# Dealing the rows of the attention's stacks into six pieces of 16 and one of 12

## The chip, the core and the metric

The kernel runs on one core of one Trainium2 chip. The time is device microseconds (us) of one launch of the whole program. The kernel before was timed three times: median 711.07 us, from 707.58 to 716.1 us. One more execution was recorded by the hardware profiler; the engines are PE (matmul), DVE (vector), ACT (scalar), POOL (GpSimd) and SP, which computes nothing here and only issues transfers (DMAs).

## The reference

Two independent halves are computed and laid side by side.

Half A is attention with a memory, on x of 2048 tokens by 576 features, with 32 heads of 18 features. The tokens are cut into 4 segments of 512. Within a segment each head does a causal softmax attention; from the second segment on, the result is mixed with what a running memory M, z of the earlier segments gives.

```python
q = heads(x @ wq); k = heads(x @ wk); v = heads(x @ wv)      # 32 heads of 18
for s in range(4):
    logits = einsum("bhqd,bhkd->bhqk", qs, ks) * scale + mask
    a_dot = einsum("bhqk,bhkd->bhqd", softmax(logits), vs)
    a_mem = einsum(phi(qs), M) / (einsum(phi(qs), z) + 1e-6)
    o = g * a_mem + (1 - g) * a_dot
    M += einsum(phi(ks), vs); z += sum(phi(ks))
out_A = concat(o) @ wo
```

Half B is a spectral filter on another x of the same size: a two-dimensional real FFT, a product with complex weights, and the inverse FFT.

## The kernel before, in words

The program has four stages, and its order of work on every engine is written out by hand (a manual schedule): what an engine gets to do is what stands next in program order.

1. **Forward FFT** of half B (`FFT.forward`), while the weights of half A are loaded and split.
2. **Projections** (`ATT.projections`, L541): for each segment g = 0..3 thirteen units. Units 0 to 8 (`qk_unit`, L467) compute 128 rows of q or k each and split them into three bf16 parts (high, middle, low). The store at L494 puts these into memory as `qkD[g]`, of 1152 rows (576 of q, then 576 of k; head h has rows 18h to 18h+17) by 3 parts by 512 tokens. Units 9 to 12 (`v_unit`, L504) compute v for 128 tokens each and store it as `vD` (L518) from `vt`, a tile of two buffers. A unit is a generator: its later steps run in later iterations, so unit 8's store to `qkD` is issued in iteration 10, and the stores to `vD` in iterations 10, 11, 12 and after the loop. Between the units the middle of the FFT runs on DVE and ACT, with its weights loaded by SP (L238). In segment 3, `hook` (L1099) also begins the inverse stage's loads on POOL and, from `q0`, the loads of the first stacks.
3. **Inverse FFT** (`FFT.inverse`, L287): matmuls at L300 and L311, stores `yb` at L320. `ATT.prologue` (L906) is interleaved: it loads the stacks of the next groups and computes the first ten rounds of `s1`.
4. **Attention** (`ATT.attention`, L928): 133 steps t. In step t, `s1(t+10)` (L637) finds the row maxima for one head of each token half, `s2(t)` (L680) computes the exponentials, and `pv` (L709) multiplies by v. Eight steps treat one group n = 0..15 (8 heads of one segment).

A **stack** is the operand of the logits' matmuls: the q (or k) of 8 heads with its bf16 parts laid one under the other in 108 of a tile's 128 partition rows, 6 parts of 18 rows, each row 8 heads by 512 tokens. There are 3 buffers for q (`Qs`) and 4 for k (`Ks`); the first of each lies in a tile called `x0`, which the profile shows as `x`. Rows 108 and 109 are written elsewhere. `stack_dmas(n,qk)` (L619) makes the loads of one stack, one per part: SP DMAs at L628, each of 18 rows times 8 heads times 512 bf16, 144 KB, read from `qkD` in runs of 1 KB. There are 32 stacks, so 192 such loads.

They are issued one by one: `hook` pops 12 of them in segment 3 of the projections (L1108), `prologue` pops 31 entries at L917, and `attention` appends 6 + 6 + 1 entries per group at L954 to L956 and pops one at L976 and one at L1005 of every step. `s1` of group n+2 begins at step 8n+6, the loads of q for that group are appended at step 8n, and those of k for group n+3 behind them. A load of a stack must wait until the last matmul that reads the buffer's old content is done. SP issues in order: whatever a DMA waits for, all later ones on SP wait too. The list `qu` (stores of the attention's results at L729 and L734, popped beside `q`) and single loads (L763, L804 and others) go through the same engine.

Of the kernel before, what the change touches and what calls it, by code (L numbers as in the profile page):

```python
# [87 lines left out]
class Pace:  # L88

    def __init__(s,total): s.left=total; s.acc=0.0; s.q=[]  # L90
# [256 lines left out]
BF=mybir.dt.bfloat16  # L347
# [42 lines left out]
class ATT:  # L390
    def __init__(s,nc,tc,io,cp,dp):
        s.nc,s.tc,s.io=nc,tc,io
        s.ident=cp.tile([128,128],F32,name="ident"); s.bm=cp.tile([126,7,19],F32,name="bm")
        s.Mst=[None]+[cp.tile([126,5,126],F32,name=f"Mst{i}") for i in range(1,4)]
        s.zst=[None]+[cp.tile([126,5,32],F32,name=f"zst{i}") for i in range(1,4)]
        d=lambda n,sh,dt: dp.tile(sh,dt,name=n)
        s.qkD=[d(f"qkD{i}",[1152,3,512],BF) for i in range(4)]
        s.pqD=[None]+[d(f"pqD{i}",[576,512],F32) for i in range(1,4)]
        s.vD=[d(f"vD{i}",[4,128,622],F32) for i in range(4)]
        s.dp=dp  # L400
# [103 lines left out]
    def v_unit(s,g,tb,tp,pp):  # L504
        nc=s.nc
        P=[]
        for hf in range(2):
            ps=pp.tile([128,288],F32,name="pjv",tag="pj")
            yield from s.passes(ps,g,"wv",slice(288*hf,288*hf+288),slice(128*tb,128*tb+128),True)
            P.append(ps)  # L510
            yield
        vt=tp.tile([128,622],F32,name="vt")
        vv=vt[:,:608].rearrange("p (h c) -> p h c",c=19)
        nc.gpsimd.memset(vv[:,:,18:19],1.0)  # L514
        nc.gpsimd.memset(vt[:,608:],0.0)
        for hf in range(2):
            nc.scalar.copy(vv[:,16*hf:16*hf+16,:18],P[hf].rearrange("p (h c) -> p h c",c=18))
        nc.sync.dma_start(s.vD[g][tb],vt)  # L518
        if g==3: return
        for _ in range(3): yield  # L520
        if tb==0: s.pm=[pp.tile([126,3,7,19],F32,name=f"pm{i}",tag="pm") for i in range(2)]
        for t in range(5):
            w=7 if t<4 else 4; r=18*w
            nc.tensor.matmul(s.pm[t//3][:r,t%3,:w].rearrange("p h c -> p (h c)"),s.pk[:,tb,126*t:126*t+r],vt[:,133*t:133*t+19*w],  # L524
                start=tb==0 and t%3==0,stop=tb==3,skip_group_check=True)
        if tb<3: return
        yield
        n=g+1
        for t in range(5):
            w=7 if t<4 else 4; r=18*w  # L530
            m=tp.tile([126,7,19],F32,name="mm")
            nc.vector.tensor_tensor(m[:r,:w],s.pm[t//3][:r,t%3,:w],s.bm[:r,:w],op=OP.mult)
            M=s.Mst[n][:r,t,:r].rearrange("p (h c) -> p h c",c=18)
            z=s.zst[n][:r,t,:w]
            if n==1:
                nc.gpsimd.tensor_copy(M,m[:r,:w,:18])
                nc.gpsimd.tensor_copy(z,m[:r,:w,18])
            else:
                nc.gpsimd.tensor_tensor(M,m[:r,:w,:18],s.Mst[g][:r,t,:r].rearrange("p (h c) -> p h c",c=18),op=OP.add)
                nc.gpsimd.tensor_tensor(z,m[:r,:w,18],s.zst[g][:r,t,:w],op=OP.add)  # L540
    def projections(s,xp,tp,pp,wv,pace,hook):  # L541

        live=[]
        s.nid=wv.tile([128,128],BF,name="nid"); s.nc.scalar.activation(s.nid,s.ident,AF.Copy,scale=-1.0)
        lw=s.load_w("wv",576,wv,xp,288,"xl",4)
        def advance():
            for l in list(live):
                try: next(l)
                except StopIteration: live.remove(l)
        tot=pace.left-8  # L550
        for g in range(4):
            if g<3: xq=[s.xprep(g+1,t,(xp,s.x0)[g%2],xp,[128,512],"xst",2) for t in range(5)]
            for i in range(13):
                u=s.qk_unit(g,i,tp,pp) if i<9 else s.v_unit(g,i-9,tp,pp)
                if i==4 and g<3: s.pk=tp.tile([128,4,576],F32,name="pk",bufs=1)
                next(u)
                hook(g,i)
                next(lw,None); next(lw,None)
                if g<3 and i in (4,6,8,10,12): next(xq[(i-4)//2])
                if g<3 and i in (1,3,5,7,9): next(xq[(i-1)//2])  # L560
                w=tot/(36-18*.3+12*2.7+4*2.0)*((2.7 if g<3 else 2.0) if i>8 else .7 if s.third(g,i) else 1.0)
                advance()
                pace.take(w*.7)
                advance()
                next(u)
                pace.take(w*.3)
                live.append(u)
        while live: advance()
# [50 lines left out]
    def stack_dmas(s,n,qk):  # L619

        nc=s.nc; g,G=divmod(n,4)
        L=[]
        T,base,order=((s.Qs[n%3],0,(0,0,0,1,1,2)),(s.Ks[n%4],576,(0,1,2,0,1,0)))[qk]
        for pc,o in enumerate(order):
            a=s.qkD[g][base+8*G*18:base+8*G*18+18,o]
            ap=bass.AP(tensor=a.tensor,offset=a.offset,ap=[[1536,18],[1536*18,8],[1,512]])
            def go(T=T,pc=pc,ap=ap):
                nc.sync.dma_start(T[18*pc:18*pc+18],ap)  # L628
                if pc==5: s.loaded.add((n,qk))
            L.append(go)  # L630
        return L
    def load_v(s,n):
# [273 lines left out]
    def prologue(s):  # L906

        nc,io=s.nc,s.io
        yield
        s.masks()  # L910
        s.load_v(0)
        q=s.stack_dmas(1,0)+s.stack_dmas(1,1)+s.stack_dmas(2,0)+s.stack_dmas(2,1)+[lambda: s.load_v(1)]+s.stack_dmas(3,1)
        for i in range(2): yield
        i=0
        for t in range(10):
            for _ in s.s1(t):
                for _ in range(1+(i%24==0)):  # L917
                    if q: q.pop(0)()
                i+=1
                yield  # L920
            if 2<=t<6: nc.gpsimd.dma_start(s.Ks[t-2][108:110].rearrange("p h c -> p (h c)"),io["neg1"])
            if t in (3,7): m=s.mpath(t//4); next(m)
            if t in (4,8): next(m); next(m,None)
        assert not q
# [151 lines left out]
def emit(nc,tc,io):  # L1076
    def pool(es,name,bufs=1,**kw):
        return es.enter_context(tc.tile_pool(name=name,bufs=bufs,reuse_waits="tile",**kw))
    with ExitStack() as L0:
# [9 lines left out]
        with tc.manual_schedule():  # L1089
            x0=pool(L1x,"x0")  # L1090
            with ExitStack() as es:
                xp=pool(es,"xf",2); cf=pool(es,"cf"); st=pool(es,"st",2)
                pf=es.enter_context(PP(tc,"pf",dict(f1=3,c1=2)))
                F.forward(xp,cf,pf,A.load_w("wqk",1152,wq,st,576,"wst",3),A.first(Slots(x0),xp),A.consts)
            with ExitStack() as es:
                wv=pool(Rv,"wv"); xp=pool(es,"xp"); tp=pool(es,"tp",2); fwp=pool(es,"fw",2)
                pp=es.enter_context(PP(tc,"pp",dict(pj=5,pt=1,pm=2)))
                F.pace.add(F.middle(fwp)); F.pace.add(F.last())
                def hook(g,i):  # L1099
                    if g==3 and i==9:  # L1100
                        Rw.close()
                        tc.swap_default_side()
                        F.yp=pool(Ri,"yp",2); F.Yt={}; ci=pool(Ri,"ci")
                        tc.swap_default_side()
                        F.inv_setup(ci)
                    if g==3 and i>9: F.ysplit(i-10,nc.vector)
                    if g==3 and i==0: q0.extend(A.stacks0(x0))
                    for _ in range((0,2,2,2,2,1,1,1,1)[i] if g==3 and i<9 else 0): q0.pop(0)()  # L1108
                q0=[]
                A.projections(xp,tp,pp,wv,F.pace,hook)  # L1110
            Rv.close()
            with ExitStack() as L1:
                cp2=pool(L1,"cp2"); sm=pool(L1,"sm",2); sp=pool(L1,"sp",3)
                ps1=L1.enter_context(PP(tc,"ps1",dict(s1=3)))
                A.begin(sm,sp,ps1)
                with ExitStack() as es:
                    pi=es.enter_context(PP(tc,"pi",dict(i2=2,i3=2,mt=1)))
                    yl=pool(es,"yl",2)
                    A.att_setup(cp2)
                    A.psm,A.mtag=pi,"mt"  # L1120
                    pr=A.prologue(); next(pr)
                    for i,_ in enumerate(F.inverse(yl,pi)):
                        if i>5 and i%4!=3: next(pr,None)
                    for _ in pr: pass
                Ri.close(); Rz.close()
                with ExitStack() as es:
                    tp=pool(es,"tp2",2); ps=es.enter_context(PP(tc,"ps",dict(s2=3,pv=1,post=1)))
                    A.attention(tp,ps)
            L1x.close()
# [18 lines left out]
```

## Time and profile before

| what | value |
|---|---|
| median of 3 runs | 711.07 us (707.58 to 716.1) |
| the profiled execution's own time | 710.93 us |
| its span, first to last instruction | 709.2 us |
| PE busy | 676.4 us, 95% of the span |
| DVE, ACT, POOL busy | 556.2, 441.0, 208.8 us |
| granted PE clock | 0.997 |
| moved by DMA | 121.04 MB, mean 171 GB/s |

The span leaves out 1.7 us of launch and end. A core has 16 DMA engines; "DMA share" is their mean busy share, so one engine always busy is 1/16. In the list of waits a row reads: engine and line that waited, what it waited for, us in total, times, longest. In the table of stretches each engine has its busy time and, in brackets, its number of instructions; the last three columns are the granted clock, the DMA share and GB/s. "SPq" is SP's instruction queue; its duration is that of issuing, not of the transfer. A wait for several things is put down to the one that came last by the profile.

### The profile page before, as it was taken

Reading aid. Unit: us, or ns where it says so; the run is one execution under the profiler, and the core shown is the slowest. Engines: PE = TensorE matmul, PEld = TensorE weight load, DVE = VectorE, ACT = ScalarE, POOL = GpSimd, SP = SyncE. Lnnn points to the kernel's source line nnn. Section 1 sums busy time; section 2 is a strip of 40 time slices with the busy share of each in tenths; the row PEclk is TensorE's granted clock in tenths of the full one; section 3 lists DMA queues with packets and bytes.
Section 4 is the critical chain, followed back from the end, with each engine's and each line's share of the span. In section 5 each row is a group of like instructions: output and inputs, shape, how many; then the busy total and the mean of one; then the engine's idle time right before and its main releaser. Section 6 shows DMA issues by size and latency. Waiting matters only on the chain.

```text
span 709.2 us, 14168 instructions
## 1 busy us (share of the span) xinstructions
PE 676.4 (95%) x4861; PEld 498.7 (70%) x4861; DVE 556.2 (78%) x1233; ACT 441.0 (62%) x994; POOL 208.8 (29%) x409
## 2 busy tenths in 40 slices
PE   4999999999999999999999899999999999998997
PEld 4999779889879888999844444444566445764677
DVE  6999999899989889887588688877666876568153
ACT  3657695574574563444388677777666676567741
POOL 2110000100100111565165334555233753246210
PEclk9999999999999999999999999999999999999999
DMA  9876546555563568899647666676556765441331
GB/s 343 272 233 205 150 141 194 175 178 167 165 211 133 165 215 279 201 239 211 180 109 176 172 161 154 173 181 169 128 129 185 171 164 128 122 129 52 99 100 69
DMA packets 83388, 121.04 MB, mean 171 GB/s; under 512 B 11368, under 2 KB 50902, under 8 KB 83180
## 3 DMA queue, kind: packets, MB, share of 16 engines
q1 hardware_dynamic: 76724, 104.11, 51.8%
q0 software_dynamic: 6592, 16.03, 8.2%
q8 instruction: 38, 0.62, 0.4%
q14 instruction: 34, 0.28, 0.1%
HBM read 81.78 MB, written 38.24 MB: 169 GB/s over the span
## 4 chain that ended last, share of the span: by engine, by line
PE 61%; DVE 9%; DMA 6%; ACT 5%; issue 3%; POOL 3%; DVEq 0%; SPq 0%; ACTq 0%; POOLq 0%
PE pv L718 9%; PE po L861 7%; PE pj L464 6%; PE pjv L464 6%; PE s L644 5%; PE i L300 4%; PE i L311 4%; PE s L652 3%; PE s L688 3%; PE po L892 2%; DVE junk L648 2%; PE s L692 2%; PE pn L791 2%; PE pm L524 2%; PE s L653 2%
## 5 line engine op out<-in xcount | busy, mean ns | idle before, releaser
L648 DVE CUSTOM_DVE_ANT_0 junk<-s,mask 128x512 bf16<-128x512 f32 (+1 forms) x256 | 141.8, 554 | 55.1 <-PE s L644 44.3
L654 DVE TENSOR_REDUCE mx<-s 128x4 f32<-128x512 f32 x128 | 87.9, 687 | 20.0 <-PE s L653 18.2
L689 ACT ACTIVATE P<-s 128x512 f32<-128x512 f32 x128 | 77.2, 603 | 24.1 <-PE s L688 20.9
L718 PE MATMUL pv<-P,vs 128*32 128x512 f32 (+3 forms) x1024 | 82.3, 440 | 0.0
L694 ACT ACTIVATE P<-s 128x512 f32<-128x512 f32 x128 | 77.1, 602 | 6.9 <-PE s L693 3.8
L698 ACT ACTIVATE P<-s 128x256 f32<-128x256 f32 x128 | 49.6, 387 | 49.7 <-PE s L697 49.6
L701 POOL TENSOR_SCALAR_AFFINE_SELECT P<-P 128x512 f32<-128x512 f32 x116 | 69.4, 635 | 5.6 <-ACT P L689 4.7
L718 PEld LDWEIGHTS pv<-P,vs 128*32 128x32 f32 x1024 | 26.9, 109 | 45.0 <-issue 42.9
L464 PE MATMUL pj<-x,wqkh 128*128 128x512 f32 x162 | 56.1, 407 | 0.0
L210 DVE TENSOR_TENSOR t<-Z 128x580 f32<-128x580 f32 x64 | 46.7, 757 | 0.2
L514 POOL MEMSET vt<- 128x32 f32 x16 | 2.4, 159 | 148.8 <-PE pm L524 121.5
L210 DVE TENSOR_TENSOR Z<-t 128x580 f32<-128x580 f32 x64 | 45.9, 756 | 0.0
L644 PE MATMUL s<-Ks,Qs 108*128 108x512 bf16 (+1 forms) x128 | 42.2, 330 | 0.0
L488 ACT CAST sp<-pj 128x512 bf16<-128x512 f32 x36 | 21.1, 585 | 30.7 <-DVE pj L484 30.7
L142 PE MATMUL f<-ftab,eh 128*128 128x290 f32 (+1 forms) x160 | 31.6, 317 | 9.0 <-DMA ftab<-ftab 9.0
L300 PE MATMUL i<-civ,Y 128*128 128x256 f32 (+1 forms) x288 | 37.9, 284 | 1.6 <-DVE T L332 1.6
L300 PEld LDWEIGHTS i<-civ,Y 128*128 128x128 f32 (+1 forms) x288 | 35.8, 181 | 1.8 <-DVE T L332 1.8
L311 PE MATMUL i<-itab,T 128*128 128x290 f32 (+1 forms) x224 | 36.4, 312 | 0.0
L464 PEld LDWEIGHTS pj<-x,wqkh 128*128 128x128 f32 x162 | 30.4, 188 | 8.4 <-issue 1.7
L669 POOL CAST mh<-mg 128x16 bf16<-128x16 f32 x32 | 6.8, 214 | 99.1 <-ACT mg L667 67.9
L464 PE MATMUL pj<-xh,wqkh 128*128 128x512 f32 x90 | 35.6, 395 | 0.0
L464 PE MATMUL pj<-xh,wqkl 128*128 128x512 f32 x90 | 35.6, 395 | 0.0
(214 smaller groups left out, 1859.6 us busy)
## 6 DMA issues: line engine op xcount, KB each, us to landing
qkD<-sp SPq DMA_DIRECT2D x36, 384.0 KB
Ks<-qkD SPq DMA_DIRECT2D x72, 144.0 KB
x<-qkD SPq DMA_DIRECT2D x60, 144.0 KB
Qs<-qkD SPq DMA_DIRECT2D x60, 144.0 KB
xin<-xb SPq DMA_DIRECT2D x16, 384.0 KB
cfw<-cfw POOLq DMA_DIRECT2D x16, 384.0 KB, 4.5
civ<-civ POOLq DMA_DIRECT2D x16, 384.0 KB, 7.5
vs<-vD SPq DMA_DIRECT2D x16, 330.0 KB
```

The costliest lines, as they stand in the source:

```text
L210: v.tensor_tensor(o,a,b,op=op)
L300: nc.tensor.matmul(p[:m,k],Y[i][:,q,c*128:c*128+m],cc[:,hl,o:o+256],start=n==0,stop=n==5)
L311: nc.tensor.matmul(p,x,t,start=n==0,stop=n==6)
L464: s.nc.tensor.matmul(out,a,b,start=i==0,stop=i==len(L)-1)
L644: nc.tensor.matmul(out,Q[:108,h,128*i:128*i+128],K[:108,h,:128*(i+1)],start=True,stop=True)
L648: nc.vector.tensor_tensor_reduce(out=junk[:,:w],in0=src,in1=s.mask[:,512-w:],scale=1.0,scalar=-3.0e38, op0=OP.add,op1=OP.max,accum_out=s.m ...
L654: nc.vector.tensor_reduce(out=s.mx[k][:,hh],in_=pa.rearrange("p (b c) -> p b c",c=128),axis=mybir.AxisListType.X,op=OP.max)
L689: nc.scalar.activation(P[0][:,hh],p0,AF.Exp,scale=SC)
L694: nc.scalar.activation(P[1][:,hh],p1,AF.Exp,scale=SC)
L701: if k<29: nc.gpsimd.affine_select(out=x,in_=x,pattern=pat+[[1,128]],compare_op=OP.is_ge,fill=0.0,base=0,channel_multiplier=-1)
L718: nc.tensor.matmul(s.pvt[32*hh:32*hh+32,128*j:],vt[:,j,19*h:19*h+32],mv[0][:,hh,mv[1]],start=j==0,stop=j==2,skip_group_check=True)
L861: nc.tensor.matmul(ps,a[t][:r,c],b[:r,t,w],start=i==0,stop=i==14)
```

## The change

A stack's six parts of 18 rows are dealt in another way: rows 0 to 15 of each part go to a piece of 16 partition rows, and the two rows left of each part, 12 in all, to a seventh piece of 12 rows. The 108 rows keep their places in q and k alike, so the sums over them are the same.

The two left-over rows of a head lie in `qkD` far from those of the other parts. They are therefore gathered in memory into a new array `reD[g]` (64 rows of 12 by 512) by `rest(g)`: 12 copies from memory to memory per segment, six for q and six for k, of 32 heads by 2 rows by 512 bf16 each. SP issues the first six at the head of iteration 11 of the projections and the other six at the head of iteration 12. The seventh piece of a stack is loaded from `reD`. The pops are adapted: two more in `hook`, a pace of `1+(i%5==0)` in place of `1+(i%24==0)` in the prologue; in the attention, the 15 entries of a group go at the same pace of two a step.

```diff
+        s.reD=[d(f"reD{i}",[64,12,512],BF) for i in range(4)]
...
+    def rest(s,g):
+
+        L=[]
+        for qk in (0,1):
+            for pc,o in enumerate(((0,0,0,1,1,2),(0,1,2,0,1,0))[qk]):
+                a=s.qkD[g][576*qk+16:576*qk+17,o]; b=s.reD[g][32*qk:32*qk+32]
+                x=bass.AP(tensor=a.tensor,offset=a.offset,ap=[[1536*18,32],[1536,2],[1,512]])
+                y=bass.AP(tensor=b.tensor,offset=b.offset+512*2*pc,ap=[[512*12,32],[512,2],[1,512]])
+                L.append(lambda x=x,y=y: s.nc.sync.dma_start(y,x))
+        return L
...
+            rest=s.rest(g)
             for i in range(13):
+                for _ in range(6 if i>10 else 0): rest.pop(0)()
...
-        for pc,o in enumerate(order):
-            a=s.qkD[g][base+8*G*18:base+8*G*18+18,o]
-            ap=bass.AP(tensor=a.tensor,offset=a.offset,ap=[[1536,18],[1536*18,8],[1,512]])
+        for pc,o in enumerate(order+(0,)):
+            if pc<6:
+                a=s.qkD[g][base+8*G*18:base+8*G*18+18,o]
+                ap=bass.AP(tensor=a.tensor,offset=a.offset,ap=[[1536,16],[1536*18,8],[1,512]])
+            else:
+                a=s.reD[g][32*qk+8*G:32*qk+8*G+8]
+                ap=bass.AP(tensor=a.tensor,offset=a.offset,ap=[[512,12],[512*12,8],[1,512]])
             def go(T=T,pc=pc,ap=ap):
-                nc.sync.dma_start(T[18*pc:18*pc+18],ap)
-                if pc==5: s.loaded.add((n,qk))
+                nc.sync.dma_start(T[16*pc:16*pc+(16 if pc<6 else 12)],ap)
+                if pc==6: s.loaded.add((n,qk))
...
-                for _ in range(1+(i%24==0)):
+                for _ in range(1+(i%5==0)):
...
-                    for _ in range((0,2,2,2,2,1,1,1,1)[i] if g==3 and i<9 else 0): q0.pop(0)()
+                    for _ in range((0,2,2,2,2,2,2,1,1)[i] if g==3 and i<9 else 0): q0.pop(0)()
```

## The prediction

> **What bounds the kernel now.** I read the page's busy times first, then the waits of PE, then the table of stretches, then SP's waits and the chain that ended last.
>
> ```profile
> PE 676.4 (95%) x4861; PEld 498.7 (70%) x4861; DVE 556.2 (78%) x1233; ACT 441.0 (62%) x994; POOL 208.8 (29%) x409
> ```
>
> PE is busy 676.4 of 709.2 us, so nothing that only makes transfers quicker can save more than PE's idle 33 us, and of these only what waits for a transfer of the stacks. In PE's waits the stacks appear once:
>
> ```profile
> PE s L652 <- DMA Ks<-qkD: 2.1, 1, 2.1
> PE i L300 <- DVE T L332: 1.6, 1, 1.6
> ```
>
> In the chain that ended last they stand near 396 us, behind loads that take 6 to 7 us each from issue to landing:
>
> ```profile
> 383.77 6.75 DMA Qs<-qkD
> 390.52 0.02 issue
> 390.54 6.15 DMA Ks<-qkD
> 396.69 0.13 issue
> 396.82 0.38 PE s L652 x2
> ```
>
> SP, which issues them, spends its time between 366 and 500 us in these waits, among others:
>
> ```profile
> SPq L628 <- PE s L697: 7.0, 5, 2.7
> SPq L628 <- DMA Ks<-qkD: 6.3, 9, 1.1
> ```
>
> A load at L628 reads memory that was written long ago. That it waits for the landing of other stack loads means that only so many transfers may be under way at once, and that the queue is full. So in this stretch the transfers run at their limit and PE is just fed. What the limit is decides the case:
>
> ```profile
> 282.00:350.00 68.00, 67.77 (x526) 64.41 (x527) 49.82 (x119) 29.99 (x74) 32.67 (x48) 1.00 0.84 210
> 366.00:400.00 34.00, 31.16 (x259) 15.63 (x260) 27.07 (x85) 25.47 (x63) 17.71 (x31) 0.97 0.71 170
> 400.00:450.00 50.00, 48.31 (x415) 23.04 (x414) 40.88 (x125) 37.54 (x93) 21.90 (x47) 0.99 0.67 160
> 450.00:500.00 50.00, 47.08 (x369) 22.23 (x367) 40.29 (x115) 36.34 (x85) 23.30 (x40) 1.00 0.70 173
> 500.00:600.00 100.00, 97.04 (x768) 55.68 (x765) 68.42 (x193) 66.91 (x157) 45.39 (x79) 1.00 0.61 150
> 404.40:412.00 7.60, 7.60 (x70) 3.83 (x69) 6.62 (x22) 5.87 (x16) 3.42 (x7) 1.00 0.63 142
> ```
> ```profile
> 257.70:258.80 1.10, 1.10 (x7) 0.87 (x6) 1.10 (x3) 0.00 (x0) 0.00 (x0) 1.00 0.43 137
> 664.90:665.60 0.70, 0.70 (x9) 0.37 (x11) 0.00 (x0) 0.34 (x2) 0.00 (x0) 1.00 0.44 105
> 131.55:132.30 0.75, 0.75 (x5) 0.61 (x4) 0.42 (x2) 0.35 (x1) 0.75 (x4) 1.00 0.89 333
> ```
>
> The second table isolates single transfers: one stack piece (18 rows), one store at L734 (also 18 rows), one store of 128 rows at L486. The 18-row ones leave over half of the 16 engines idle (shares 0.43 and 0.44). GB/s divided by share times 16 is what one busy engine moves: 19.9 for the piece alone, 14.9 for the 18-row store, 23.4 for the 128-row store, and in 404.4 to 412, where almost only stack pieces fly one behind another, 14.1.
>
> **The change, part by part.** *The pieces.* A row of a piece carries 8 x 1,024 = 8,192 bytes whatever the number of rows. Two limits are possible, and they bound the cost.
>
> (a) Rows are the limit. In the full queue 142 GB/s over 18 rows is 7.9 GB/s a row, so a piece takes 8,192 / 7,900 = 1.04 us with 18, with 16 or with 12 rows. A stack goes from 6 x 1.04 = 6.2 us to 7 x 1.04 = 7.3 us: +1.04 us.
>
> (b) Engines are the limit. If the 16 rows are spread over all 16 engines, each at the 23.4 GB/s of the 128-row store, a piece of 131,072 bytes takes 131,072 / 374,000 = 0.35 us, a stack 2.5 us: -3.8 us.
>
> I take (a). An engine that moves these same 1 KB runs at 19.9 GB/s when a piece is alone falls to 14.1 when pieces queue behind one another; and the store, of as few rows, has 14.9. The engines could do more; what these slow cases share is that few rows of the tile are touched. The row at 404.4 us is also the nearest: same line, same runs, 18 rows against 16.
>
> The Trainium skill states such a rule (SBUF — State Buffer, "Door 1: The DMA port swizzle"): a transfer's bandwidth goes by how many of the memory's 16 ports its partitions reach, four neighbouring partitions share one, and partitions 0 to 15 measured 104 GB/s at 1 MiB. By that figure, as an estimate, a 16-row piece would take 1.26 us, a stack 8.8, and the sum below would come to about 745. The trace agrees with the rule's kind but lies above its rate: 142 GB/s on 18 rows, where 4.5 ports would give about 122.
>
> *How full the queue is.* The loads issued in these stretches, in the order 366 to 400, 400 to 450, 450 to 500:
>
> ```profile
> x<-qkD SPq DMA_DIRECT2D x12, 144.0 KB
> ...
> Qs<-qkD SPq DMA_DIRECT2D x6, 144.0 KB
> Ks<-qkD SPq DMA_DIRECT2D x6, 144.0 KB
> ```
> ```profile
> Qs<-qkD SPq DMA_DIRECT2D x12, 144.0 KB
> Ks<-qkD SPq DMA_DIRECT2D x12, 144.0 KB
> x<-qkD SPq DMA_DIRECT2D x11, 144.0 KB
> ```
> ```profile
> Qs<-qkD SPq DMA_DIRECT2D x12, 144.0 KB
> Ks<-qkD SPq DMA_DIRECT2D x12, 144.0 KB
> x<-qkD SPq DMA_DIRECT2D x7, 144.0 KB
> ```
>
> That is 24, 35 and 31 pieces. For 400 to 450: 35 x 1.04 = 36.4 us. All bytes are 160 x 50 = 8.0 MB, the pieces 35 x 0.147 = 5.2 MB, so 2.8 MB are others; at the 210 GB/s of the mixed traffic in 282 to 350 they take 13.5 us. Together 49.9 of 50 us. In the same way 25.0 + 10.7 = 35.7 of 34, and 32.2 + 19.4 = 51.6 of 50: full, within the coarseness of this. For 500 to 600 (53 pieces):
>
> ```profile
> Ks<-qkD SPq DMA_DIRECT2D x23, 144.0 KB
> Qs<-qkD SPq DMA_DIRECT2D x18, 144.0 KB
> x<-qkD SPq DMA_DIRECT2D x12, 144.0 KB
> ```
>
> 55.1 + 34 = 89 of 100 us, so 11 us are free.
>
> *The price.* A sixth more pieces of equal time is 90 / 6 x 1.04 = 15.6 us more in 366 to 500. From this goes what SP spent waiting for PE to free a stack's buffer (7.0 us): there the queue could not be served earlier and has air. That leaves +8.6 us, which falls on PE at L652 as longer waits for the last piece of q. In 500 to 600, 53 / 6 x 1.04 = 9.2 us fit into the 11 free: 0, up to +4.6 if half of it does not fit. In 282 to 350 the 30 pieces become 35, +5.2 us, hidden by PE's own work (67.77 of 68 us busy) because groups 1 and 2 are loaded a whole stage ahead; up to +5.2 if the stores at L320, queued behind the pieces on SP, hold up the output tiles.
>
> *The copies of `rest`.* For 48 copies and 32 more pieces SP issues some 80 times 0.33 us. In segments 0 to 2 the copies lie beside PE's and DVE's work; SP gets to the next store 2 us later, and the two buffers of `vt` leave a unit of time: 0, or 2 us a segment if that cover is gone. In segment 3 it is not so:
>
> ```profile
> 270.27 0.32 SPq L494
> ...
> 270.69 6.88 DMA vD<-vt
> ...
> 277.67 0.06 ACT vt L517
> ...
> 282.15 1.93 PE i L300 x14
> ```
>
> In this chain the second `vD` store's landing releases ACT's copy into `vt`, behind which ACT's cast for the inverse stage and so PE stand. Six copies of 0.32 us each are put ahead of that store: +2.0 us. Bounds: 0 if the landing goes by the crowd of other transfers and not by the issue, +3.8 if the 0.39 MB of the six copies delay it too (at the 210 GB/s above, 1.8 us). The other six copies must wait for the last `qkD` store to land (6 to 7 us, if it takes as long as its neighbour in the chain), and behind them stand the last two `vD` stores and the loads of mask and beta; these are first read at L652, from 288.4 us on:
>
> ```profile
> L652 PEldq EVENT_SEMAPHORE  x49: 51/51/3347, 286.3 to 626.8; - x49
> L652 PE MATMUL s<-x x32: 217/271/339, 288.4 to 577.2; 108*128 108x384 bf16 x16, 108*128 108x128 bf16 x16
> ```
>
> That is 6 us after PE resumes at 282.15, with the same delay in it: 0.
>
> *Matmuls*: unchanged in number and shape, 0. PE looks at one more semaphore per stack (0.051 us by the first row above, 32 x 0.051 = 1.6 us in all), ahead of the matmul that needs it: 0, up to 1.6 if nothing were ahead.
>
> *Sum:* 710.93 (the profiled execution, 0.14 below the median of the runs) + 8.6 + 2.0 = 721.5 us.
>
> **The rivals.** *A, engines are the limit: 709 us.* Pieces take 0.35 us, the queue empties, the wait of 2.1 us at 396 goes, and the copies cost 0 to 2.0: 708.8 to 710.8. For it: over half of the engines idle for a piece alone, and that piece at 19.9 GB/s an engine. Against it: 14.1 in the full queue. It decides if a 16-row piece takes under 6/7 of an 18-row one. More than the 2.1 us could come only from waits that the profile puts down to other causes. The Trainium skill speaks for this rival's first half (DMA: Bandwidth & Descriptors, "Why a DMA increments its semaphore by 16 and not by 1"): the number of engines is the largest up to 16 that divides the slowest dimension, 9 for 18 rows and 16 for 16. The share of 0.43 and 0.44 agrees with 9/16 = 0.56 as the ceiling.
>
> *B, the whole second half is bound by the queue: 735 us.* No air is used (15.6 in place of 8.6), the inverse stage adds 5.2, 500 to 600 half of its 9.2, less 3.0 of waits that overlap: 710.93 + 15.6 + 5.2 + 4.6 + 2.0 - 3.0 = 735. For it: the sums of 366 to 500 are full already. Against it: PE's one wait of 2.1 us, so much is loaded early enough.
>
> *C, pieces of 16 rows take less in proportion and only the copies cost: 714 us.* A piece of 16 rows at 16/18 of 1.04 us and the one of 12 at 12/18 keep a stack at 6 x 16/18 + 12/18 = 6 such times, 6.2 us as before (the limit is then bytes, not rows); the copies add 2.0 to 3.8: 712.9 to 714.7. For it: the bytes are the same. Against it: the 18-row store gives 105 GB/s where the pieces give 142, so bytes per second are no constant.
>
> **How the numbers follow.** Forecast 721.5: 0.48, its own range 715 to 730. A 0.30, B 0.12, C 0.10. A change of under 1%, 7 us, can hardly be told from none with this kernel. Of the forecast's 0.48 I give 0.41 to slower by more than that (above 718.2) and 0.07 to within; B is slower; C within; of A 0.20 within and 0.10 faster, for gains that no row shows. Faster 0.10, same 0.37, slower 0.53. The range runs from A less 3 us of scatter (the lowest run lies 3.5 below the median), 706, to B and 3 us, 738.
>
> **What would show it.** Right: in a stretch with only stack pieces the DMA share rises to 0.8 or more while GB/s stays at 110 to 145; PE's waits at L652 for `qkD` or `reD` loads grow from 2.1 to some 10 us, between 366 and 500; the first matmul of the inverse stage after its wait (282.15) comes 0 to 4 us later. Wrong: GB/s in such a stretch above 200 and SP's waits for landings gone (A); the waits of PE unchanged with SP's waits as before (C); waits for `yb` or after 500 us (B).

## The result, and the profile after

The changed kernel takes 715.42 us (median of 20 runs, 712.28 to 719.42) against 711.41 us (707.51 to 716.35) for the kernel before on the same chip: a ratio of 1.0059, 95% interval 1.0035 to 1.0082, so 0.4 to 0.8% slower. Its profiled execution took 714.65 us with a span of 712.9 us, 3.7 us more than the one before. The forecast was 721.5 us, 10.6 us more than before; about 4 us came. All ratios and intervals here are those on record: they leave disturbed runs out and are not the quotients of the medians beside them, from which they differ by up to 0.23%.

First the busy time of PE and then its waits, from the page and the list of waits of the changed kernel:

```profile
PE 677.5 (95%) x4861; PEld 500.4 (70%) x4861; DVE 555.8 (78%) x1233; ACT 440.9 (62%) x994; POOL 209.1 (29%) x409
```
```profile
PE i L300 <- DVE T L332: 4.0, 1, 4.0
...
PE s L669 <- DMA Ks<-qkD: 1.5, 2, 1.3
```

PE waits no longer for the stacks than before: 1.5 us in all, against 2.1 in one wait. What grew is its gap at the inverse stage (L300, waiting for DVE's `T`), from 1.6 to 4.0 us. That place has nothing to do with the stacks. The chain that ended last, from there backwards in time (start, us, what):

```profile
271.33 6.28 DMA qkD<-sp
...
277.63 0.53 SPq L550
...
280.76 0.59 SPq L550
...
281.41 0.03 SPq L519
...
281.46 3.22 DMA vD<-vt
...
284.87 0.70 DVE T L332
...
285.62 4.21 PE i L300 x18
```

L550 issues the copies of `rest`. The six for k wait until the last `qkD` store has landed (277.6), then keep SP until 281.4, and only behind them goes the `vD` store. The tile `T` of the inverse stage lies in memory that `vt` had, so DVE's write of it waits for that store, and PE waits for DVE. The row at 285.62 holds a second loss: 18 matmuls take 4.21 us, where the kernel before took 2.40 us in its chain (`282.15 2.40 PE i L300 x18`). The table of stretches around it (the third column from the right is the granted clock):

```profile
281.46:284.87 3.41, 0.17 (x2) 0.00 (x0) 0.94 (x2) 1.20 (x4) 2.77 (x4) 1.00 0.83 257
284.87:288.28 3.41, 2.66 (x12) 2.67 (x13) 1.12 (x2) 0.00 (x0) 0.03 (x1) 0.50 0.99 246
288.28:291.70 3.42, 3.42 (x17) 3.42 (x16) 1.12 (x2) 2.13 (x6) 1.46 (x2) 0.50 0.44 139
291.70:295.11 3.41, 3.41 (x30) 3.28 (x29) 1.93 (x4) 1.45 (x3) 0.82 (x2) 1.00 0.46 127
```

Behind the gap PE runs for 6.8 us at half its clock, with 29 matmuls in the two stretches where the next one has 30 alone. Last, the stretches of the second half in which the forecast saw the loss:

```profile
366.00:400.00 34.00, 33.09 (x288) 16.11 (x290) 28.68 (x93) 27.85 (x69) 20.72 (x34) 1.00 0.78 158
400.00:450.00 50.00, 47.70 (x413) 23.05 (x406) 40.36 (x123) 36.15 (x90) 20.55 (x42) 1.00 0.96 162
450.00:500.00 50.00, 46.76 (x363) 22.39 (x363) 40.75 (x117) 37.32 (x89) 25.66 (x46) 1.00 0.92 177
500.00:600.00 100.00, 97.01 (x775) 54.03 (x772) 70.23 (x200) 67.67 (x159) 43.56 (x76) 1.00 0.78 151
```

From 400 to 500 us the DMA share went from 0.67 to 0.70 up to 0.92 to 0.96, while GB/s stayed (160 and 173 before, 162 and 177 now) and PE is as busy as it was (94.5 us of 100, before 95.4).

Where the 3.7 us arise can be read from single matmuls: how much later than before the same one starts. "Stack n" stands from here on for the two stacks, q and k, of group n.

| | before | after | later by |
|---|---|---|---|
| the inverse stage goes on (L300) | 282.15 | 285.62 | 3.5 |
| first matmul of stack 0 (L652, now L669) | 288.43 | 294.58 | 6.2 |
| first matmul of stack 4 | 396.82 | 402.15 | 5.3 |
| first matmul of stack 5 | 413.88 | 418.12 | 4.2 |
| last matmul | 705.09 | 708.80 | 3.7 |

By the first matmul of stack 0 6.2 us are lost, and 2.5 us of them come back later: the wait before stack 4 is 1.3 us in place of 2.1, and the half clock that followed it in the kernel before (397.7 to 401.1 us, shown in the last section) is not there.

### The profile page after: what moved, and what is told of

It is laid out like the page before. It is cut to its first block, busy times and chain, and to the rows that moved or that the text cites. A ratio compares the mean times of both kernels' runs of the same rounds, so it can differ in the third digit from the quotient of the medians.

```text
span 712.9 us, 14250 instructions
## 1 busy us (share of the span) xinstructions
PE 677.5 (95%) x4861; PEld 500.4 (70%) x4861; DVE 555.8 (78%) x1233; ACT 440.9 (62%) x994; POOL 209.1 (29%) x409
## 4 chain that ended last, share of the span: by engine, by line
PE 63%; DVE 12%; DMA 9%; ACT 8%; issue 4%; POOL 2%; SPq 1%; DVEq 0%; ACTq 0%; POOLq 0%
PE pv L735 9%; PE po L878 7%; PE pj L465 6%; PE pjv L465 6%; PE s L661 5%; PE i L300 4%; PE i L311 4%; PE s L669 3%; PE s L705 3%; PE po L909 2%; PE s L709 2%; DMA qkD<-sp 2%; PE pn L808 2%; PE c L163 2%; PE pm L525 2%
## 5 line engine op out<-in xcount | busy, mean ns | idle before, releaser
L300 PE MATMUL i<-civ,Y 128*128 128x256 f32 (+1 forms) x288 | 39.6, 292 | 4.0 <-DVE T L332 4.0
L300 PEld LDWEIGHTS i<-civ,Y 128*128 128x128 f32 (+1 forms) x288 | 37.4, 189 | 4.2 <-DVE T L332 4.2
```

The source lines that it names most:

```text
L300: nc.tensor.matmul(p[:m,k],Y[i][:,q,c*128:c*128+m],cc[:,hl,o:o+256],start=n==0,stop=n==5)
```

## The experiments

Theory 1: the copies hold the last `vD` stores of segment 3, PE stands idle at the inverse stage, and the half clock doubles the price. Theory 2, the forecast's: seven pieces take longer in the queue than six. The ratios are each against the kernel before on the same chip.

| kernel | median us | ratio | 95% interval |
|---|---|---|---|
| copies_only | 713.94 | 1.0046 | 1.0022 to 1.0071 |
| deal_only | 712.86 | 1.0025 | 1.0001 to 1.0050 |
| late_copies | 720.74 | 1.0127 | 1.0083 to 1.0171 |
| k_late | 716.12 | 1.0076 | 1.0043 to 1.0108 |
| behind | 711.51 | 1.0005 | 0.9984 to 1.0026 |
| pause | 716.71 | 1.0075 | 1.0047 to 1.0104 |
| warm | 715.31 | 1.0062 | 1.0038 to 1.0085 |
| nine | 723.52 | 1.0159 | 1.0123 to 1.0196 |
| pq_early | 714.34 | 1.0051 | 1.0024 to 1.0077 |
| pq_late | 713.86 | 1.0020 | 0.9989 to 1.0050 |
| behind_early | 710.15 | 0.9975 | 0.9947 to 1.0003 |

**Each half of the change alone.** `copies_only` is the kernel before with the copies issued and never read; `deal_only` is the changed kernel without the copies: its seventh piece reads 12 rows of another part, so it leaves out the left-over rows.

> The copies alone, at their places in the change; the stacks are loaded as before in six pieces of 18 rows, and nothing reads what the copies write. Theory 1 (the copies of segment 3 delay the v stores, PE idles 4 us at the start of the inverse stage and the granted clock then falls to one half for some us): 2.4 + 2.7 us above the kernel before, ratio 1.005 to 1.009, and a stretch at half clock near 285 us. Theory 2 (the 32 more pieces fill the queue): ratio 0.999 to 1.002.

> The dealing alone, without copies: the seventh piece reads 12 rows of another part from the old array, so it moves the same bytes with the same runs, and the sums over the stacks are wrong. Theory 1: no idle of PE above 2 us near 282, ratio to before 0.995 to 0.999 (some 2 us less, since the wait near 396 us shrinks and its half-clock stretch goes). Theory 2: still slower, ratio 1.003 or more.

The copies alone cost 0.2 to 0.7%, the seven pieces 0.0 to 0.5%. The forecast's +8.6 us (1.2%) for the pieces is excluded. The two intervals overlap, so this pair alone doesn't divide the loss: `copies_only` came out just under what theory 1 gave for it, and `deal_only` between the two expectations, closer to theory 2's.

**The copies of segment 3 elsewhere.** Three places were tried. The first, all twelve behind the prologue, and the second, the six for k alone behind it:

```diff
-                for _ in range(6 if i>10 else 0): rest.pop(0)()
+                for _ in range(6 if i>10 and g<3 else 0): rest.pop(0)()
...
                     for _ in pr: pass
+                    for f in A.rest(3): f()
```

> The change with the twelve copies of segment 3 issued after the prologue (near 350 us), where SP is little used. Theory 1: as the dealing alone, 709 us, ratio to before 0.995 to 0.999. Theory 2: as the change, ratio 1.004 to 1.008.

> The change with only the six k copies of segment 3 issued after the prologue; the six q copies stay ahead of the second v store. Theory 1 as the trace of the change has it (the k copies wait for the last store to qkD and hold the third v store): PE resumes near 282 to 283, ratio 0.995 to 1.000. If the q copies do the harm, as the prediction had it: ratio 1.003 or more.

Both missed: `late_copies` is slower than the changed kernel (1.0059), `k_late` no faster. By its number alone `k_late` would speak for the copies of q; its profile does not. The step that theory 1 named did happen, and another wait took its place. PE at the inverse stage, and later the chain that ended last:

```profile
282.77 1.46 PE L300 MATMUL i<-civ,Y 128*128 128x256 f32 x10 [1.63 <-DVE T L332]
```
```profile
352.52 0.74 SPq L550
...
355.87 0.59 SPq L550
...
356.50 0.59 SPq L652
...
357.14 0.03 SPq L624
...
357.20 5.01 DMA ob<-wo
...
362.24 0.67 ACT woh L628
```

PE's gap is 1.6 us again and it goes on at 282.77. But at the new place the copies stand ahead of the loads of `wo` on SP; ACT's cast of `wo` waits for these, its exponentials stand behind the cast, and PE had a gap of 2.5 us at 361 us, with the half clock behind it from 363.6 to 367.0 us. That the same holds for `late_copies` is argued, not shown: no profile of it is used here.

The third place is right behind the first load of v, where SP issues nothing from 281.0 to 287.5 us in the kernel before:

```diff
         s.masks()
         s.load_v(0)
+        for f in s.rest(3): f()
```

> The changed kernel with all twelve copies of segment 3 moved: they are issued right behind the first load of v in the prologue, where SP has nothing to do for 9 us. Theory 1 (the copies ahead of segment 3's last v stores hold PE for 4.0 us at the start of the inverse stage, and the half clock behind that idle costs as much again): PE's gap before the inverse stage is 1.6 us again as in the kernel before, no stretch at clock 0.50 follows it, and the time is near that of the kernel with the pieces alone, 712.9 (712 to 713.5). Theory 2 (the 32 more pieces in the queue cost the time): the time stays at the changed kernel's 715.4, with the gap gone and PE's waits at the loads of the stacks grown instead.

Theory 1 holds: 1.0005 (711.51 us, a little under its 712 to 713.5), no difference from the kernel before, with all 48 copies and the seven pieces still there. The gap in PE's order of work:

```profile
282.59 2.41 PE L300 MATMUL i<-civ,Y 128*128 128x256 f32 x18 [1.57 <-DVE T L332]
```

The 18 matmuls take 2.41 us, at full clock. So the place of twelve copies makes the difference between 1.0059 and 1.0005, and what the dealing and the other 36 copies cost in `behind` is at most 0.26%, 1.9 us, and not distinguishable from nothing. `deal_only`, with 1.0001 at the lower end of its interval, leaves room for a small price of the dealing.

**The half clock.** Two runs ask what it follows. `pause` is the kernel before with DVE work in front of the same `T`, no copies, no new pieces; `warm` is the changed kernel with PE busy in the gap:

```diff
+                if u==1:
+                    z=s.Z[:,0,0]
+                    for z in (z,z,z,z[:,0]): v.tensor_tensor(z,z,z,op=OP.max)
                 v.tensor_tensor(l,p,h[:,:2].bitcast(F32),op=OP.subtract)
```
```diff
+            if u==2:
+                d=pp.tile([128,512],F32,name="wm",tag="mt")
+                for _ in range(20): nc.tensor.matmul(d[:,:FP],tab[:,0,0,0,:128],tab[:,0,0,0],start=True,stop=True)
```

> The kernel before, no copies and no smaller pieces; four operations on data that nobody reads any more are put on DVE ahead of the second T of the inverse stage, 2.4 us in all, so that PE's gap there grows from 1.6 to 4.0 us. Theory 1 (an idle PE alone brings the half clock): 6.8 us at clock 0.50 follow, as in the changed kernel, and the time goes to 714.6 to 716.5 (2.4 for the gap, 2.7 for the clock, less up to 1.9 that the loads of the stacks gain). Rival (the half clock comes from what the DMAs or the copies do): the clock stays at 1.00 there and the time is 711.4 to 713.8.

> The changed kernel; 20 matmuls whose result nobody reads (2.7 to 2.9 us) are put on PE into its 4.0 us gap before the inverse stage. The copies, the pieces and the late landing of v stay. Theory 1 (idle of PE above some 2 us brings the half clock): the gap left is about 1.1 us, no clock of 0.50 behind it, and the time falls by up to 2.7 us to 712.7 to 714. Rival (the half clock comes from the DMA traffic of that moment, or is a price of the late v stores): clock 0.50 for 6.8 us as before and 715.4.

`pause` on PE, then `warm` on PE:

```profile
286.30 3.86 PE L300 MATMUL i<-civ,Y 128*128 128x256 f32 x18 [4.71 <-DVE T L335]
```
```profile
282.29 2.89 PE L328 MATMUL wm<-itab 128*128 128x290 f32 x20
286.78 2.40 PE L300 MATMUL i<-civ,Y 128*128 128x256 f32 x18 [1.61 <-DVE T L335]
```

In `pause` the gap became 4.7 us, 0.7 more than meant, and the half clock followed with no copy in sight: 18 matmuls took 3.86 us, and the kernel was 0.5 to 1.0% slower. In `warm` the gap left was 1.6 us, 0.5 more than meant, and the 18 matmuls took 2.40 us, at full clock, with all the copies there. So an idle PE brings the half clock. The length was not as expected: 3.4 us in `pause` after the longer gap, 6.8 us in the changed kernel (the last section has the reason as far as the traces show it).

The time of `warm` missed its forecast: 1.0062, nothing gained. Its profile shows two reasons. The last copies on SP took longer in this run, `281.26 1.77 SPq L553` in its chain, and PE went on 1.2 us later than in the changed kernel (286.78 against 285.62). And the wait before stack 4 took the rest, 2.25 us with a half clock behind it:

```profile
397.80:401.20 3.40, 1.58 (x19) 0.50 (x18) 1.68 (x6) 1.33 (x4) 0.41 (x2) 1.00 0.98 163
401.20:404.60 3.40, 2.98 (x13) 1.74 (x14) 1.74 (x4) 1.46 (x4) 0.00 (x0) 0.50 0.81 192
```

Stack 0 began 1.5 us earlier than in the changed kernel (293.06 against 294.58), stack 4 only 0.5 us earlier (401.62 against 402.15), and with the half clock behind it: its loads gain little when PE is early, so time won ahead of it is given back there.

**The price of a piece.** `bench18` puts loads of this form alone on SP behind the kernel's end:

```diff
+            def blk(j,ts,rows,order=None):
+                for T in ts:
+                    for p in (order or range(108//rows)):
+                        r=min(rows,108-rows*p); a=A.qkD[0][0:18,0]
+                        nc.sync.dma_start(bt[T][rows*p:rows*p+r],bass.AP(tensor=a.tensor,offset=a.offset,ap=[[1536,r],[1536*18,8],[1,512]]))
+                nc.sync.dma_start(sc[j:j+1],bt[ts[-1]][90:91,0,:8])
+            blk(0,(0,1),18); blk(1,(2,3),16,range(7)); blk(2,(4,5),16,(0,2,1,3,4,6,5)); blk(3,(6,),8,range(13)); blk(4,(7,8),32,range(3))
```

> The kernel before with a tail behind its end, in which SP alone issues loads of the stacks' form into buffers that nobody reads: 12 of 18 rows, 14 of 16 rows (two of them 12) in order, the same 14 with neighbours swapped, 14 of 8 rows (one of 4), 6 of 32 rows. Forecast's step (rows are the limit: 1.04 us a piece whatever its rows): GB/s goes with the rows, 142 at 18, 126 at 16, 63 at 8, 250 at 32. Rival C (bytes per second are the limit): the same GB/s, 140 to 160, in all, and only the DMA share goes up with the number of engines. Rival A (the number of engines is the limit): 16 rows give more than 18, 200 GB/s or more.

The edit issues 13 pieces of 8 rows, not 14. All its loads read from the same place in `qkD[0]`, which those of the stacks do not, and there is one execution of it.

The middle of each block, in this order: 18 rows, 16 rows, 16 rows with neighbours swapped, 8 rows, 32 rows (the last two columns are the DMA share and GB/s; the compute engines are idle). A share above 1 cannot be busy time alone, so it is read here only as the time that the packets took:

```profile
708.50:720.00 11.50, 0.00 (x0) 0.00 (x0) 0.00 (x0) 0.00 (x0) 0.00 (x0) 0.50 0.62 135
724.00:735.00 11.00, 0.00 (x0) 0.00 (x0) 0.00 (x0) 0.00 (x0) 0.00 (x0) 0.50 1.11 130
739.00:752.50 13.50, 0.00 (x0) 0.00 (x0) 0.00 (x0) 0.00 (x0) 0.00 (x0) 0.50 1.08 109
756.50:763.50 7.00, 0.00 (x0) 0.00 (x0) 0.00 (x0) 0.00 (x0) 0.00 (x0) 0.50 0.55 96
767.50:773.00 5.50, 0.00 (x0) 0.00 (x0) 0.00 (x0) 0.00 (x0) 0.00 (x0) 0.50 1.12 210
```

With 8,192 bytes a row, a piece of 18 rows takes 147,456 bytes / 135 GB/s = 1.09 us, one of 16 rows 1.01 us, one of 12 at the same rate 0.76 us, one of 8 rows 0.68 us, one of 32 rows 1.25 us. None of the three theories fits all of it: GB/s neither goes with the rows nor stays the same over the whole range, and a larger share (1.11 against 0.62) brings no more of them. Between 18 and 16 rows, though, it is nearly the same, and that is the step in question: a stack goes from 6 x 1.09 = 6.5 us to 6 x 1.01 + 0.76 = 6.8 us, +0.26 us and not +1.04. The blocks as wholes can't be compared: the first 18-row loads share the queue with the last stores of the kernel's results (236 GB/s from 705.75 to 708.5 us, where the stretch above has 135).

**More and smaller pieces.** Was the rest of the forecast's step sound, that the excess falls on PE? `nine` loads each piece of 18 rows as two of 9:

```diff
-                nc.sync.dma_start(T[18*pc:18*pc+18],ap)
+                for j in range(2): nc.sync.dma_start(T[18*pc+9*j:18*pc+9*j+9],ap[j])
```

> The kernel before with each piece of 18 rows loaded as two of 9 rows: the same bytes, rows and places in SP's order, no copies. The loads of that form measured by themselves take 1.09 us for 18 rows and 0.68 us for 8, so a stack goes from 6.5 to some 8.2 to 8.7 us. If the forecast's step is right in kind (the queue is full between 366 and 500 us, and what goes beyond SP's 7.0 us of air falls on PE), the 15 stacks there need 25 to 33 us more, and the time is 729 to 737. If PE is served early enough and the queue has more air than SP's waits show, it stays below 720.

It costs 1.59% (1.23 to 1.96%), 11.3 us, between the two expectations. SP's waits at the stack loads, in `nine` and then in the kernel before:

```profile
SPq L628 <- DMA Qs<-qkD: 28.6, 69, 2.0
SPq L628 <- DMA Ks<-qkD: 15.1, 32, 1.6
SPq L628 <- DMA x<-qkD: 14.7, 35, 1.1
```
```profile
SPq L628 <- DMA Ks<-qkD: 11.4, 14, 2.0
SPq L628 <- DMA Qs<-qkD: 8.5, 9, 2.2
SPq L628 <- DMA x<-qkD: 4.4, 5, 1.6
```

From 24.3 us in 28 waits to 58.4 us in 136. So a queue that takes longer for a stack does reach PE, though by about half of what the forecast's way of counting gives (25 to 33 less 7.0 us of air: 18 to 26). In the changed kernel the same waits did not grow. These are the three longest of five rows; with `x<-qkD` and `Ks<-reD`, 0.8 us each, they come to 7.2 us in 17 waits:

```profile
SPq L645 <- DMA Ks<-qkD: 2.7, 7, 0.9
SPq L645 <- DMA Qs<-qkD: 2.0, 4, 0.8
...
SPq L645 <- DMA Qs<-reD: 0.9, 2, 0.6
```

That is less than the 24.3 us before, where seven pieces of unchanged time would have made it more. The loads are also issued at another pace in the changed kernel, so how much of the fall is due to the pieces is not shown.

**Can the wait before stack 4 go?** The five loads of `pq` stand among stack 4's loads. They were issued earlier, later, and earlier in the kernel with the copies well placed:

```diff
-            if 16<=t<21: s.pq_load(1,t-16)
+            if 11<=t<16: s.pq_load(1,t-11)
```

> The kernel before with the five loads of pq for group 1 (0.26 MB each, first read at 422 us) issued five steps earlier, so that they no longer stand among the loads of stack 4 that PE waits for at 396 us. If that wait of 2.1 us and the half clock of 3.4 us behind it come from these loads, both go and the time falls by up to 3.8 us, to 707 to 709. Rival: the wait has its cause in the queue as a whole and comes back at the next stack; then the time is as before, 710 to 711.

> The same with these five loads ten steps later than in the kernel before, just ahead of their first use. If the wait at 396 us comes from them, it goes here too, and the time is 707 to 709 unless they now come late for PE's matmuls at 422 us; rival as in the run with the early loads: 710 to 711.

> The changed kernel with segment 3's copies behind the first load of v in the prologue and the five loads of pq five steps earlier. If the pieces of 16 rows cost nothing and the two waits come from the places of the copies and of these loads, it is as fast as the kernel before with the early loads, 707 to 709.5. If the dealing costs by itself, it is slower than that one by 1 us or more.

The first missed (1.0051, slower): in its profile the wait before stack 4 was 3.0 us in place of 2.1. The second gained nothing (1.0020, with 1 inside the interval). In the profile of `pq_late` stack 4 starts without a wait, and a new one arises some 65 us on:

```profile
394.77 0.38 PE L652 MATMUL s<-x,Qs 108*128 108x384 bf16 x2
```
```profile
460.39 0.38 PE L824 MATMUL pb<-rr,sel 96*126 96x512 bf16 x1 [1.67 <-DMA rr<-rrD]
```

The rival fits better: moving a load moves the wait or lengthens it, and does not remove it. `behind_early`, 710.15 us, is the fastest median of all, but its interval (0.9947 to 1.0003) reaches 1, and in its profile the wait before stack 4 was 2.8 us with a half clock behind it: the early loads did not remove it there either. That it is faster than `pq_early` with the same early loads (0.9975 against 1.0051) speaks against any price of the pieces of 16 rows. No version beats the kernel before measurably.

## Why the prediction was wrong

*"I take (a)": a stack goes "from 6 x 1.04 = 6.2 us to 7 x 1.04 = 7.3 us".* This is the step that failed. A piece of 16 rows does not take as long as one of 18: 1.01 against 1.09 us, measured by themselves. With +0.26 in place of +1.04 us a stack the same sum gives 90 / 6 x 0.26 = 3.9 us, less than the 7.0 us of air, so 0; and in the kernel `behind` leaves at most 1.9 us for the pieces, where the forecast had 8.6. That was rival C's account of the pieces, which had a chance of 0.10; its 2.0 to 3.8 us for the copies stood at the wrong six, as in the forecast. The reading behind it, that engines standing idle mean that the rows are the limit, is only half right: the idle engines were indeed no reserve (share up, GB/s the same), but that excludes the engines and doesn't yet make the time of a piece independent of its rows. The mark chosen for it, a share of 0.8 or more at 110 to 145 GB/s where only pieces of stacks are under way, came true in the changed kernel, here where almost only such pieces are:

```profile
410.00:415.00 5.00, 5.00 (x45) 2.59 (x44) 4.48 (x14) 3.90 (x11) 2.96 (x7) 1.00 1.15 139
```

It could not tell (a) from C: at 16 rows (a) gives 126 GB/s and C 142, and both lie inside the mark. The other mark, PE's waits at the loads of the stacks growing to some 10 us, did not come.

*The excess less the air falls on PE.* Right in kind, as `nine` shows, and too high by about half.

*"Six copies of 0.32 us each are put ahead of that store: +2.0 us."* A copy takes SP 0.59 us, and these six keep SP for 3.8 us; yet PE went on at 282.77 in `k_late`, which has them there, and at 282.59 in `behind`, which does not: 0.2 us.

*"The other six copies ... : 0".* The second step that failed. It said that the last two `vD` stores stand behind these copies, and then asked only who reads mask and beta. The one who waits for the last `vD` store is the writer of `T`, in the memory that `vt` leaves. Cost: 285.62 against 282.59 in `behind`, 3.0 us, and the half clock behind it, which the prediction did not have: stack 0 starts 5.7 us later than in `behind` (294.58 against 288.88).

*500 to 600 us: 0.* Right: PE is busy for 97.01 us there, before 97.04.

So the sum had the wrong 8.6 us and left out what came, and the 2.0 us stood at the wrong six copies. That the kernel got slower and that 715.4 us lies inside the stated 715 to 730 is luck, not the forecast's mechanism; so is the 3.5 us by which the inverse stage went on later, inside the 0 to 4 that it gave for the other six copies. Of the measured 0.59%, `behind` leaves 0.05% when twelve copies are moved: that cause is shown. Not shown is how much of `copies_only`'s 0.46% arises at the same place, no profile of which is used here.

## What to carry to other kernels

When instructions are put into a queue, list everything behind them up to the next idle time of the queue, stores too, and ask of each store who writes into the memory that it reads: a store that nobody reads soon can still hold an engine. The price of a transfer of another shape is measured by itself before it is multiplied by 90; idle DMA engines alone say neither that there is a reserve nor what else the limit is. A wait that puts PE to rest for some 2 us or more can cost the half clock on top, so a new wait is priced at up to twice its length, and a time that is won ahead of a later wait may be given back there.

## What the runs showed of the hardware

**The clock goes by stretches of 3.41 us.** Between the kernel's first and last microseconds, every half clock in the profiles used here lasted 3.4 or 6.8 us. Cut at that length, the table shows what came ahead of it (first column after the stretch's length: PE busy; third from the right: the granted clock). The kernel before, `pause`, and `deal_only`, in this order; the changed kernel's and `warm`'s stand above:

```profile
394.29:397.70 3.41, 1.35 (x16) 0.69 (x9) 0.86 (x6) 0.60 (x3) 0.41 (x2) 1.00 0.62 164
397.70:401.11 3.41, 3.41 (x17) 1.59 (x18) 2.84 (x8) 2.55 (x6) 1.24 (x2) 0.50 0.63 178
401.11:404.52 3.41, 3.41 (x34) 1.78 (x26) 2.06 (x6) 2.18 (x7) 1.85 (x3) 1.00 0.76 189
```
```profile
279.90:283.31 3.41, 1.68 (x15) 1.45 (x13) 3.31 (x7) 1.82 (x4) 2.35 (x2) 1.00 0.82 203
283.31:286.73 3.42, 0.43 (x3) 0.43 (x4) 3.26 (x5) 0.00 (x0) 1.36 (x3) 1.00 0.80 230
286.73:290.14 3.41, 3.41 (x18) 3.41 (x17) 0.60 (x1) 1.19 (x3) 0.00 (x0) 0.50 0.23 77
290.14:293.55 3.41, 3.41 (x29) 3.41 (x28) 1.76 (x5) 1.34 (x5) 2.28 (x3) 1.00 0.01 2
```
```profile
394.30:397.75 3.45, 1.93 (x21) 0.63 (x19) 2.04 (x8) 1.69 (x5) 0.42 (x2) 1.00 0.94 145
397.75:401.16 3.41, 2.82 (x21) 1.62 (x25) 2.08 (x6) 2.08 (x6) 0.30 (x1) 1.00 0.78 183
```

A stretch with PE busy for 0.17, 0.43, 1.35 or 1.58 us was followed by one at 0.50; after 1.68 and 1.93 us none came. (`deal_only` has no half clock near; its stretches are counted back from the one at its end, at 708.4 us.) In `nine`, though, one came after 1.74 us. So the limit lies near half of a stretch, not sharp in PE's busy time as the profile has it, and the same gap can cost nothing or 1.7 us by how it falls on the stretches: `deal_only`'s gap of 2.1 us fell on two of them and was free, the 2.06 us of the kernel before fell into one and was not. In the changed kernel the rest of the gap fell into the second stretch, PE was busy for only 2.66 us of it at half clock, and the third was slow too; in `pause` the second was full and the clock came back, and in `warm` 2.98 of 3.40 us were enough for that. That is the difference between 6.8 and 3.4 us. The Trainium skill (TensorE: Matmul & The Clock Gate, "Part 1: The HAM clock gate") states a window of 3,413 ns that runs freely and a half clock after at least one idle window. The length agrees with these traces; the window need not be idle, one in which PE was busy for 1.58 of 3.40 us was enough.

**GB/s of small pieces.** Swapping neighbours among pieces of 16 rows, so that rows 0 to 15 and rows 32 to 47 follow one another, lowered GB/s from 130 to 109, the form and the number being the same, in the one execution of `bench18`. The Trainium skill (SBUF — State Buffer, "Door 1: The DMA port swizzle") lets partitions 32 apart share a port, which would make such neighbours collide. The traces agree with that, and with its rule that more ports give more (96, 130, 210 GB/s for 8, 16, 32 rows), though not in proportion.

**Issuing a copy.** The chains above show 0.59 us of SP for one copy from memory to memory. A stack's load, here in `behind`, keeps it about half as long, and the prediction had taken one price for both:

```profile
390.37 0.31 SPq L645 DMA_DIRECT2D Ks<-qkD  x1
```
